# Expert leftovers in half tiles: two column groups on TensorE and a switch of seven arms

## The chip, the core and the metric

The kernel runs on one core of one Trainium2 chip. The metric is the device time of one execution in microseconds (us), lower being better; the profile adds one execution taken apart instruction by instruction. Engines are named as the profile names them: PE (TensorE, the matrix engine), PEld (its weight loads), DVE (VectorE), ACT (ScalarE), POOL (GpSimd) and SP (SyncE).

## The reference

The program is a strided sparse attention followed by a mixture of experts with one expert per token. Attention works on 8 batches, 8 heads, 576 positions and 64 channels a head; its output, reshaped to 8 x 576 rows of 512 floats, is the input of the expert layer:

```python
for b in range(B):
    prev_e = -1
    for s in range(S):
        fresh_e = int(np.argmax(logits[b, s]))
        if s == 0 or local_gate[b, s] < 0.5:
            e = fresh_e
        else:
            e = prev_e if prev_e >= 0 else fresh_e
        prev_e = e
        ls = logits[b, s] - logits[b, s].max()
        p = np.exp(ls)
        p /= p.sum() + 1e-09
        h = np.maximum(x[b, s] @ w1[e], 0.0)
        out[b, s] = p[e] * (h @ w2[e])
```

There are 8 experts; `w1[e]` is 512 x 1024 and `w2[e]` is 1024 x 512, all in float32. How many of the 4608 rows an expert gets depends on the data. Routing the given inputs by the reference gives 701, 469, 606, 495, 656, 452, 546 and 683 rows for experts 0 to 7.

## The kernel before, in words

Attention runs first, for about 190 us, and writes the rows to `xd` in DRAM. The router sorts rows by expert into tiles of 128 rows and keeps for each slot the row number and its gate. Then the expert stage runs; this is where the change lies.

**Units of work.** A *pair* is two tiles, 256 rows. `pair_hidden` and `pair_output` compute it with seven block products instead of eight, from sums of weights and of rows. In the hidden product (L807) the stationary operand is a 128 x 128 block of `w1` or of a weight sum, and the moving operand is 128 transposed rows. In the output product (L843) the hidden rows are stationary and 256 columns of `w2` move. A *single* (`single`) is one tile without the seven-product scheme: 32 matmuls of 128 columns for the hidden layer (L898) and 8 of 512 columns for the output (L909). A float32 matmul appears in the profile as two instructions, a transpose as one.

**Around a unit.** `gather` (L737) fetches its rows from `xd` by an indirect DMA that POOL issues, `scale` (L743) multiplies them by the gate on ACT, `turn` (L750, L751) transposes them on PE and copies them to `xt` on ACT, `row_sums` (L759) makes row sums for a pair on DVE, and `scatter` (L763) writes the result rows by an indirect DMA, again issued by POOL. `scale` and `turn` of the next unit are called inside the unit before it, so that the next rows are ready when it starts; a unit's transposes are therefore found among the matmuls of its predecessor.

**Four certain tiles, then a switch.** Every expert does its first two pairs (tiles 0 to 3). What lies past four tiles is known only at run time: `Router.arms` computes `pick`, the number of tiles past the fourth, held to 0 to 3. `choose` loads it into the registers of PE, ACT, DVE and POOL, and `rest` opens a switch in the middle of the second pair's output. The arms are written out in full: arm 0 nothing, arm 1 a single, arm 2 a pair, arm 3 a pair and a single. With the counts above, experts 0, 4 and 7 take arm 2, experts 2 and 6 take arm 1, and experts 1, 3 and 5 take arm 0. Expert 1 is finished before expert 0; the others follow in order.

**Order.** The order within each engine is that of the program text. Each unit calls `run(steps)` at set places; these steps are the DVE sums of the next expert's weights. The weights of the next expert are loaded by SP into one of two sets of buffers when the expert that used that set has finished with it. The rows of an expert's second pair and of its leftovers share one buffer; the first pair of the next expert has another.

Of the kernel before, what the change touches and what calls it, by code (L numbers as in the profile page):

```python
# [8 lines left out]
F32 = mybir.dt.float32  # L9
BF16 = mybir.dt.bfloat16  # L10
I32 = mybir.dt.int32
Act = mybir.ActivationFunctionType
Alu = mybir.AluOpType
# [5 lines left out]
P = 128  # L19
B, H, S, DH = 8, 8, 576, 64  # L20
D = H * DH
E, F = 8, 1024
DK, FK = D // P, F // P
N = B * S
# [16 lines left out]
HALF = P // 2  # L41


XT = 7
# [10 lines left out]

WARM = 14

ARMS = 4
SKIP = 8192
NEG = -8.0e9  # L60

# [21 lines left out]
class Unit:  # L83


    def __init__(self, b, pair, g):
        self.b, self.pair, self.g = b, pair, g
        self.local = pair < PAIRS // 2
        self.w, n = (LQ, LT) if self.local else (SQ, ST)
        self.kb = LK if self.local else SQ  # L90
        self.m = n // 2
# [356 lines left out]
class Router:  # L448
# [200 lines left out]
    def arms(self, bank):  # L649

        nc, pool, R, ident = self.nc, self.pool, self.R, self.ident
        f = lambda name, shape, t=F32: pool.tile(shape, t, name=name)
        ti, pk, ov, fine, bad = f("ti", [E, 1], I32), f("pk", [E, 1]), f("ov", [E, 2]), f("fine", [P, 2]), f("bad", [1, 1])

        nc.vector.tensor_scalar(ti, self.total[0:E], float(P), None, Alu.add)
        nc.vector.tensor_scalar(ti, ti, 7, None, Alu.arith_shift_right)
        nc.vector.tensor_copy(pk, ti)
        nc.vector.tensor_scalar(ov[:, 0:1], pk, -float(XT), 0.0, Alu.add, Alu.max)
        nc.vector.memset(ov[:, 1:2], 1.0)
        nc.vector.tensor_scalar(pk, pk, -4.0, 0.0, Alu.add, Alu.max)  # L660
        nc.vector.tensor_scalar(pk, pk, float(XT - 4), None, Alu.min)

        nc.vector.tensor_scalar(self.good, self.sums, 1.0 / TRUST, None, Alu.is_ge)
        nc.vector.scalar_tensor_tensor(self.good, self.sums, TRUST, self.good, Alu.is_le, Alu.mult)
        nc.vector.tensor_reduce(fine[:, 0:1], self.good.rearrange("p n h i -> p (n h i)"), axis=AX.X, op=Alu.min)
        nc.vector.memset(fine[:, 1:2], 1.0)
        yield
        ps = bank()
        nc.tensor.matmul(ps[0:1, 0:E], lhsT=pk, rhs=ident[0:E, 0:E], start=True, stop=True, skip_group_check=True)
        nc.tensor.matmul(ps[0:1, E:E + 1], lhsT=ov[:, 0:1], rhs=ov[:, 1:2], start=False, stop=True, skip_group_check=True)  # L670
        nc.vector.tensor_copy(self.pick, ps[0:1, 0:E])
        nc.tensor.matmul(ps[0:1, E + 1:E + 2], lhsT=fine[:, 0:1], rhs=fine[:, 1:2], start=False, stop=True,
                         skip_group_check=True)
        nc.vector.tensor_scalar(bad, ps[0:1, E + 1:E + 2], -1.0, float(P), Alu.mult, Alu.add)
        nc.vector.tensor_tensor(bad, ps[0:1, E:E + 1], bad, op=Alu.add)
        nc.vector.tensor_copy(self.flag, bad)
        yield
# [37 lines left out]
class Rows:  # L715


    def __init__(self, spot, tab, gi, cols, rows=N):
        self.x, self.xt, self.t = spot
        self.rows = rows  # L720
        self.n = len(cols)
        self.si = [tab[:, j, 0:1] for j in cols]
        self.gate = [tab.bitcast(F32)[:, j, 1:2] for j in cols]
        self.gi = [gi[:, j:j + 1] for j in cols]


class Experts:
# [6 lines left out]

    def gather(self, r):
        for i in range(r.n):
            self.nc.gpsimd.indirect_dma_start(out=r.x[:, i], out_offset=None, in_=self.xd[0:r.rows],  # L737
                                              in_offset=bass.IndirectOffsetOnAxis(ap=r.gi[i], axis=0))

    def scale(self, r):  # L740
        if r is not None:
            for i in range(r.n):
                self.nc.scalar.activation(r.x[:, i], r.x[:, i], Act.Copy, scale=r.gate[i])  # L743

    def turn(self, r, bank, only=None):
        if r is not None:
            for i in range(r.n) if only is None else [only]:
                ps = bank()[:, 0:DK * P].rearrange("p (k x) -> p k x", k=DK)
                for kk in range(DK):
                    self.nc.tensor.transpose(ps[:, kk], r.x[:, i, kk * P:(kk + 1) * P], self.ident)  # L750
                self.nc.scalar.copy(out=r.xt[:, i], in_=ps)  # L751

    def row_sums(self, r, which=range(4)):
        if r is not None and r.n == 2:
# [6 lines left out]
    def scatter(self, y, i, r):  # L761

        s = self.nc.gpsimd.indirect_dma_start(  # L763
            out=self.out, out_offset=bass.IndirectOffsetOnAxis(ap=r.si[i], axis=0),
            in_=y[:, i], in_offset=None, bounds_check=N - 1, oob_is_err=False)
        self.tc.declare_no_dep(s.ins, group="out", reason="scatters write different rows")
        self.tc.add_to_no_dep_group("out", s.ins)

    def run(self, ctx):
        nc, tc, w1, w2, router = self.nc, self.tc, self.w1, self.w2, self.router  # L770
        new = lambda name, bufs, **k: ctx.enter_context(tc.tile_pool(name=name, bufs=bufs, reuse_waits="tile", **k))
        wp, xp, up = new("wp", 1), new("xp", 1), new("up", 1)
        psx, psl, psm = new("psx", 2, space=PSUM), new("psl", 3, space=PSUM), new("psm", 1, space=PSUM)
# [3 lines left out]
        spots = [self.spot, (xp.tile([P, 2, D], F32, name="x1"), *self.spot[1:])]  # L777
        state = {"flip": 0}
# [4 lines left out]
        def run(steps):  # L783
            for do in steps.pop(0) if steps else []:
                do()
# [3 lines left out]
        def u(name, shape, pool=up):  # L789
            if name not in kept:  # L790
                kept[name] = pool.tile(shape, F32, name=name)
            return kept[name]

        relu = lambda o, i: nc.scalar.activation(o, i, Act.Relu)  # L794
        add = lambda o, i, p: nc.vector.tensor_tensor(o, p, i, op=Alu.add)  # L795
        hs, ys = [P, 4, P], [P, 256]
# [113 lines left out]
            nc.scalar.copy(out=y[:, 0], in_=ps)  # L910
            self.scatter(y, 0, r)

        def rows(spot, e, tiles):
            return Rows(spots[spot], router.tab, router.gi, [t * E + e for t in tiles])

        def load(e, w):
            w.load(nc, w1, w2, e)
            return w.sums(nc.vector)

        def slots(todo, counts):  # L920

            return [[todo.pop(0) for _ in range(min(n, len(todo)))] for n in counts]

        def output(r, w, h, nxt, steps):
            part1, part2 = pair_output(r, w, h)
            part1(steps)
            part2(nxt, steps)

        def choose(e):
            value = nc.values_load(router.pick[0:1, e:e + 1], engines=ENG, min_val=0, max_val=ARMS - 1,  # L930
                                   skip_runtime_bounds_check_because="held between 0 and 3")
            index = {n: value for n in ENG}
            tc.switch_hint(index, ARMS, label=f"expert{e}")
            return index

        def rest(e, w, spot, second, index, steps, nxt):

            if nxt is not None:
                self.gather(nxt)
            part1, part2 = pair_output(second, w, pair_hidden(second, w, steps))  # L940
            part1(steps)
            flip = state["flip"]

            for arm in tc.Switch(index, ARMS, hint=f"expert{e}"):
                state["flip"] = flip
                left = list(steps)
                more = []
                if arm > 1:
                    more.append(rows(spot, e, (4, 5)))
                if arm % 2:  # L950
                    more.append(rows(spot, e, (3 + arm,)))
                if more:
                    self.gather(more[0])
                part2(more[0] if more else nxt, left)
                for i, r in enumerate(more):
                    then = more[i + 1] if i + 1 < len(more) else nxt
                    if i + 1 < len(more):
                        self.gather(then)
                    if r.n == 1:
                        single(r, w, then, left)  # L960
                    else:
                        output(r, w, pair_hidden(r, w, left), then, left)
                while left:
                    run(left)
# [7 lines left out]
        more = router.scatters(1)  # L972
# [7 lines left out]
        arms = router.arms(bank)  # L980
        places[3].append(lambda: next(arms))
        places += [[lambda: next(arms), router.table, lambda: self.gather(second)]]
        h = pair_hidden(other, W[1], places)
        router.fetch()
        output(other, W[1], h, second, places)
        nxt = rows(1, 0, (2, 3))
# [4 lines left out]
        nxt = rows(0, 2, (0, 1))  # L991
        rest(0, W[0], 1, second, index, slots(sums, [0, 0, 1, 2, 1, 2, 2, 2, 2]) + [[f] for f in sums], nxt)
        for e in range(2, E):
            w, first, steps = W[(e + 1) % 2], nxt, []
            second = rows(1, e, (2, 3))
            self.gather(second)
            if e + 1 < E:
                steps = slots(load(e + 1, W[e % 2]), [0] * 5 + [1, 1, 1, 3] + [1] * 8 + [2])
                nxt = rows(0, e + 1, (0, 1))
            else:  # L1000
                nxt = None
            h = pair_hidden(first, w, steps)
# [466 lines left out]
```

## Time and profile before

| what | value |
|---|---|
| time, median of 9 runs | 744.96 us (741.96 to 752.91) |
| time of the profiled execution | 743.47 us |
| its span in the profile | 741.7 us |
| granted PE clock, mean | 0.961 |
| PE busy | 697.1 us, 94% of the span |
| PEld busy | 621.4 us, 84% |
| DVE busy | 380.9 us, 51% |
| ACT busy | 198.9 us, 27% |
| POOL busy | 134.1 us, 18% |
| DMA | 95.83 MB, mean 129 GB/s |

The profiled time is the span and 1.77 us around it. In the rows of the profile a group is the instructions of one source line, engine and shape: `L909 PE MATMUL mps<-w2t,h 128*128 128x512 f32 x32` is line 909, a matmul into the tile `mps`, with a 128 x 128 stationary block and 512 moving columns, executed 32 times. A matmul's own duration includes its latency; consecutive matmuls overlap, so what one costs in a stream is the distance between starts.

### The profile page before, as it was taken

The page shows a single profiled execution, that of the slowest core. Times are in us where ns is not written, and L with a number is a line of the kernel's source. Part 1 is how long each engine was busy: PE and PEld are TensorE (multiplying, and loading weights), DVE is VectorE, ACT ScalarE, POOL GpSimd, SP SyncE. Part 2 cuts the span into 40 slices and gives each one's busy share as a digit, 9 for nine tenths or more (in the row PEclk, how much of TensorE's full clock was granted, in tenths as well). Part 3 has the DMA queues.
Part 4 walks back from the last instruction along what each step waited for, and adds up shares of the span by engine and source line. Part 5 has one row for each costly group of instructions (what it writes and reads, how often), then busy time and mean ns, then how long its engine had stood idle before and what let it go on. Part 6 is the DMA issues. An engine that isn't in the chain of part 4 may idle for free.

```text
span 741.7 us, 15189 instructions
## 1 busy us (share of the span) xinstructions
PE 697.1 (94%) x6170; PEld 621.4 (84%) x6170; DVE 380.9 (51%) x896; ACT 198.9 (27%) x360; POOL 134.1 (18%) x150
## 2 busy tenths in 40 slices
PE   8999998697898999999999999999999999999993
PEld 5887886485697788999998999999999999889992
DVE  6667765372474523574563257366436646324341
ACT  3444452241320122221222222222222222212320
POOL 3000003204047221211121121131012112111001
PEclk9999999696998799999999999999999999999998
DMA  9798888722530024505222512520161442010000
GB/s 325 276 364 271 292 278 253 218 79 63 173 117 30 20 70 137 180 30 184 97 73 104 196 58 99 189 87 31 51 224 58 138 146 74 31 36 31 30 29 27
DMA packets 38057, 95.83 MB, mean 129 GB/s; under 512 B 5358, under 2 KB 14574, under 8 KB 37888
## 3 DMA queue, kind: packets, MB, share of 16 engines
q1 hardware_dynamic: 29616, 73.77, 29.0%
q0 software_dynamic: 7744, 20.08, 8.5%
q8 instruction: 64, 1.05, 0.6%
q14 instruction: 105, 0.86, 0.4%
q10 hardware_dynamic: 528, 0.07, 0.1%
HBM read 74.93 MB, written 20.02 MB: 128 GB/s over the span
## 4 chain that ended last, share of the span: by engine, by line
PE 90%; issue 3%; DVE 3%; DMA 1%; ACT 1%; POOL 1%; another core or an unknown queue 0%; POOLq 0%
PE lps L807 33%; PE mps L843 31%; PE sps L252 6%; PE vps L276 6%; PE tps L317 3%; PE xps L750 2%; PE lps L898 2%; PE mps L909 2%; PE sps L246 2%; PE vps L354 1%; PE tps L336 1%; DMA qk<-in_qks_dram 1%; DMA x<-xd,gi 1%; DVE xl L290 1%; DVE sums L289 0%
## 5 line engine op out<-in xcount | busy, mean ns | idle before, releaser
L807 PE MATMUL lps<-tt,ws 128*128 128x128 f32 x912 | 109.7, 275 | 3.8 <-issue 3.7
L807 PEld LDWEIGHTS lps<-tt,ws 128*128 128x128 f32 x912 | 105.6, 192 | 4.1 <-issue 3.9
L763 POOL DMA_INDIRECT out_dram<-y,tab x40 | 45.9, 1146 | 332.1 <-DVE y L795 273.4
L843 PE MATMUL mps<-wt,k 128*128 128x256 f32 x456 | 101.6, 379 | 0.0
L843 PEld LDWEIGHTS mps<-wt,k 128*128 128x128 f32 x456 | 86.6, 190 | 11.8
L795 DVE TENSOR_TENSOR h<-lps,u 128x512 f32<-128x512 f32 x57 | 39.4, 691 | 77.7 <-PE lps L807 69.9
L807 PE MATMUL lps<-xt,w1t 128*128 128x128 f32 x608 | 75.9, 279 | 0.0
L807 PEld LDWEIGHTS lps<-xt,w1t 128*128 128x128 f32 x608 | 74.1, 196 | 1.9 <-issue 1.0
L843 PE MATMUL mps<-w2t,h 128*128 128x256 f32 x304 | 72.5, 382 | 0.0
L577 POOL DMA_INDIRECT slots<-tok,idx x40 | 40.7, 1018 | 143.8 <-DVE tok L568 131.6
L843 PEld LDWEIGHTS mps<-w2t,h 128*128 128x128 f32 x304 | 56.9, 192 | 7.1
L252 PE MATMUL sps<-qk 64*128 64x96 f32 (+2 forms) x704 | 55.8, 286 | 5.8 <-issue 5.2
L737 POOL DMA_INDIRECT x<-xd,gi x40 | 39.6, 990 | 113.5 <-DVE tab L637 28.7
L252 PEld LDWEIGHTS sps<-qk 64*128 64x128 f32 (+2 forms) x704 | 45.4, 186 | 16.6 <-issue 14.4
L794 ACT ACTIVATE h<-h 128x512 f32<-128x512 f32 x57 | 35.9, 630 | 83.3 <-DVE h L795 81.3
L256 ACT ACTIVATE e<-sps 128x576 f32<-128x576 f32 (+1 forms) x64 | 41.4, 651 | 56.0 <-PE sps L252 34.3
L795 DVE TENSOR_TENSOR u<-lps,p 128x512 f32<-128x512 f32 x19 | 13.1, 692 | 58.3 <-PE lps L807 49.0
L807 PE MATMUL lps<-tt,w1t 128*128 128x128 f32 x304 | 40.8, 285 | 2.4 <-issue 2.4
L794 ACT ACTIVATE h<-lps 128x512 f32<-128x512 f32 x23 | 13.7, 597 | 104.8 <-PE lps L807 64.2
L807 PEld LDWEIGHTS lps<-tt,w1t 128*128 128x128 f32 x304 | 37.5, 198 | 4.4 <-issue 3.9
L807 PE MATMUL lps<-xt,ws 128*128 128x128 f32 x304 | 39.0, 284 | 0.0
L843 PE MATMUL mps<-w2t,k 128*128 128x256 f32 x152 | 37.6, 392 | 0.0
(214 smaller groups left out, 913.5 us busy)
## 6 DMA issues: line engine op xcount, KB each, us to landing
w1t<-in_w_dram SPq DMA_DIRECT2D x8, 2048.0 KB
w2t<-in_w_dram SPq DMA_DIRECT2D x8, 2048.0 KB
qk<-in_qkl_dram SPq DMA_DIRECT2D x16, 592.0 KB
qk<-in_qks_dram SPq DMA_DIRECT2D x16, 576.0 KB
vl<-in_vf_dram SPq DMA_DIRECT2D x8, 780.0 KB
vs<-in_vg_dram SPq DMA_DIRECT2D x8, 639.8 KB
xd<-xl SPq DMA_DIRECT2D x16, 288.0 KB
xd<-xs SPq DMA_DIRECT2D x64, 63.0 KB
```

Of the source, the lines that this page charges most:

```text
L246: nc.tensor.matmul(ps[0:GK, h, 0:n], lhsT=identb[0:GK, 0:GK], rhs=maskS[:, 0:n], start=True, stop=False, skip_group_check=True)
L252: nc.tensor.matmul(ps[0:m, h, c:c + w], lhsT=t[r, S + j * width:S + j * width + m], rhs=t[r, j * width:j * width + w], start=(u.local and ...
L256: nc.scalar.activation(e[0:kb, :, 0:n], ps[0:kb, :, 0:n], Act.Exp, bias=0.0, scale=1.0 / DH ** 0.5)
L276: nc.tensor.matmul(ps[a * HALF:(a + 1) * HALF, h, i], lhsT=u.e[0:m, h, q0:q0 + HALF], rhs=vt[0:m, j, 2 * i2 + h], start=(i == 0 and h == 0 ...
L317: nc.tensor.transpose(ps[:, t], src[:, t], ident)
L577: s = self.nc.gpsimd.indirect_dma_start(out=self.T, out_offset=bass.IndirectOffsetOnAxis(ap=self.idx[0:m, t, b:b + 1], axis=0), in_=self.t ...
L737: self.nc.gpsimd.indirect_dma_start(out=r.x[:, i], out_offset=None, in_=self.xd[0:r.rows], in_offset=bass.IndirectOffsetOnAxis(ap=r.gi[i], ...
L763: s = self.nc.gpsimd.indirect_dma_start(out=self.out, out_offset=bass.IndirectOffsetOnAxis(ap=r.si[i], axis=0), in_=y[:, i], in_offset=Non ...
L794: relu = lambda o, i: nc.scalar.activation(o, i, Act.Relu)
L795: add = lambda o, i, p: nc.vector.tensor_tensor(o, p, i, op=Alu.add)
L807: nc.tensor.matmul(ps[:, f], lhsT=m[:, kk, f * P:(f + 1) * P], rhs=v[:, kk], start=(start and f == 0 and kk == 0), stop=(kk == 1), skip_gr ...
L843: nc.tensor.matmul(ps[:, 0:256], lhsT=m[:, f], rhs=v[:, f], start=(start and f == 0), stop=(f == 3), skip_group_check=True)
```

## The change

`pick` now counts half tiles (64 rows) past the eighth, held to 0 to 6, and the switch has seven arms:

| arm | rows past 512 | work |
|---|---|---|
| 0 | none | nothing |
| 1 | up to 64 | a half |
| 2 | up to 128 | a single |
| 3 | up to 192 | a single and a half |
| 4 | up to 256 | a pair |
| 5 | up to 320 | a pair and a half |
| 6 | up to 384 | a pair and a single |

With the counts above, experts 0, 4 and 7 (189, 144 and 171 rows past 512) take arm 3, expert 2 (94 rows) takes arm 2, expert 6 (34 rows) takes arm 1, and experts 1, 3 and 5 take arm 0.

A *half* is a new unit of 64 rows. Its rows are the stationary operand in both products. Sixty-four stationary columns fill half of the array, so each product is split into two column groups: group 0 writes PSUM partitions 0 to 63 and group 1 partitions 64 to 127. In the hidden product group `g` has columns `512 g` to `512 g + 511` of `w1` as its moving operand; in the output product it has columns `256 g` to `256 g + 255` of `w2`. Between them the hidden rows are transposed on PE and copied back to SBUF by DVE. Gather, scale, transposes and scatter of a half work on 64 rows.

```diff
-ARMS = 4
+ARMS = 7
...
-        nc.vector.tensor_scalar(ti, self.total[0:E], float(P), None, Alu.add)
-        nc.vector.tensor_scalar(ti, ti, 7, None, Alu.arith_shift_right)
+        nc.vector.tensor_scalar(ti, self.total[0:E], float(HALF), None, Alu.add)
+        nc.vector.tensor_scalar(ti, ti, 6, None, Alu.arith_shift_right)
...
-        nc.vector.tensor_scalar(pk, pk, -4.0, 0.0, Alu.add, Alu.max)
-        nc.vector.tensor_scalar(pk, pk, float(XT - 4), None, Alu.min)
+        nc.vector.tensor_scalar(pk, pk, -8.0, 0.0, Alu.add, Alu.max)
+        nc.vector.tensor_scalar(pk, pk, float(ARMS - 1), None, Alu.min)
...
+        def half(r, w, nxt, steps):
+
+            self.scale(nxt)
+            a = psl.tile(hs, F32, name="lps").rearrange("p k x -> p (k x)")
+            for kk in range(DK):
+                for g in range(2):
+                    nc.tensor.matmul(a[g * HALF:(g + 1) * HALF], lhsT=r.xt[:, 0, kk, 0:HALF],
+                                     rhs=w.w1[:, kk, g * 512:(g + 1) * 512], start=(kk == 0), stop=(kk == DK - 1),
+                                     skip_group_check=True)
+            h, ht = u("h22", hs), u("h12", hs)
+            relu(h.rearrange("p k x -> p (k x)"), a)
+            self.turn(nxt, bank)
+            ps = psl.tile(hs, F32, name="lps")
+            for f in range(4):
+                nc.tensor.transpose(ps[:, f], h[:, f], self.ident)
+            nc.vector.tensor_copy(ht, ps)
+            self.row_sums(nxt)
+            flip = state["flip"] = 1 - state["flip"]
+            y = u(f"y{flip}", [P, 2, D])
+            b = u("mps0", [P, 512], psm)
+            for f in range(FK):
+                for g in range(2):
+                    nc.tensor.matmul(b[g * HALF:(g + 1) * HALF, 0:256], lhsT=ht[:, f % 4, f // 4 * HALF:(f // 4 + 1) * HALF],
+                                     rhs=w.w2[:, f, g * 256:(g + 1) * 256], start=(f == 0), stop=(f == FK - 1),
+                                     skip_group_check=True)
+            while steps:
+                run(steps)
+            for g in range(2):
+                nc.scalar.copy(out=y[0:HALF, 0, g * 256:(g + 1) * 256], in_=b[g * HALF:(g + 1) * HALF, 0:256])
+            self.scatter(y, 0, r)
...
-                if arm > 1:
+                if arm > 3:
                     more.append(rows(spot, e, (4, 5)))
+                if arm % 4 > 1:
+                    more.append(rows(spot, e, (4 + arm // 4 * 2,)))
                 if arm % 2:
-                    more.append(rows(spot, e, (3 + arm,)))
+                    more.append(rows(spot, e, (4 + arm // 2,), HALF))
...
-                    if r.n == 1:
+                    if r.m < P:
+                        half(r, w, then, left)
+                    elif r.n == 1:
                         single(r, w, then, left)
```

The rest of the diff passes the number of rows of a unit, 128 or 64, to `gather`, `scale`, `turn` and `scatter`.

## The prediction

> **What bounds the kernel now.** I read the page first: engine shares and the chain that ended last.
>
> ```profile
> span 741.7 us, 15189 instructions
> PE 697.1 (94%) x6170; PEld 621.4 (84%) x6170; DVE 380.9 (51%) x896; ACT 198.9 (27%) x360; POOL 134.1 (18%) x150
> PE 90%; issue 3%; DVE 3%; DMA 1%; ACT 1%; POOL 1%; another core or an unknown queue 0%; POOLq 0%
> ```
>
> PE carries 90% of the chain. A share is an average over stages, so next I read the chain in order of time where expert 2 ends. Columns are start, duration, what, number of instructions.
>
> ```profile
> 370.58 12.51 PE lps L807 x112
> 383.09 10.36 PE mps L843 x48
> 393.45 0.44 PE xps L750 x4
> 393.89 1.73 PE mps L843 x8
> 395.62 7.14 PE lps L898 x64
> 402.76 0.87 PE xps L750 x8
> 403.63 6.87 PE mps L909 x16
> ```
>
> Each piece starts where the last ended: from 297 us to the end of the last pair no other engine holds the chain. What counts here is the sum of PE's slots, so a unit's price is its slots plus any wait it brings. A pair costs 12.51 + 10.36 + 1.73 plus 0.87 for its own eight transposes, 25.47 us. The single costs 7.14 + 6.87 + 0.44 (four transposes, at 393.45), 14.45 us. The 0.87 at 402.76 belongs to the next pair and stays. Slots: 6.87 / 16 = 429 ns for 512 moving columns, 10.36 / 48 = 216 ns for 256, 7.14 / 64 = 112 ns for 128, 0.87 / 8 = 109 ns for a transpose.
>
> The half depends on two column groups running at once. Attention already does that twice, so I read PE's timeline there, and the row of line 336 (minimum, median and maximum ns, then its shapes).
>
> ```profile
> 65.31 0.77 PE L317 MATMUL tps<-ident,xs 128*128 128x128 f32 x5
> 66.00 1.62 PE L276 MATMUL vps<-vl,e 128*64 128x65 f32 x48
> 67.55 1.18 PE L336 MATMUL tps<-xT,wgs 128*32 128x504 f32 x16
> 68.66 0.43 PE L246 MATMUL sps<-maskS,identb 126*126 126x252 bf16 x2
> ```
>
> ```profile
> L336 PE MATMUL tps<-xT,wgs x128: 226/457/1049, 30.0 to 191.6; 128*32 128x504 f32 x64, 128*32 128x72 f32 x64
> ```
>
> L276 writes two groups of 64 columns. At about 60 ns a slot (112 ns less 63 columns at (216 - 112) / 128 ns) 48 of them would take 2.9 us one by one; the next line starts after 1.55. Its two groups share one moving block. L336 is nearer to the half: four groups of 32 columns, each with a different block of `xT` moving, half the instructions of 504 columns. One by one that is 8 x 423 + 8 x 65 ns = 3.9 us; the next line starts after 1.11. Four at a time it would be 0.98. So groups with different long moving operands do overlap fully.
>
> **The change, part by part.** *Streams of the half.* The hidden product is 8 matmuls, 16 instructions of 512 columns; two at a time, 8 x 429 ns = 3.44 us (6.87 one by one). The output product is 32 instructions of 256; two at a time, 16 x 216 = 3.45 us (6.91 one by one). I take the full overlap of L336. What neither row shows is a group that accumulates over its blocks; full-width streams (L898, L909) do so at an unbroken pace.
>
> The Trainium skill has a rule that speaks against this: "TensorE: Matmul & The Clock Gate", section "Measured speedup vs the span model", gives 2.38 times for three column groups of 32 with 512 columns, 0.79 of the ideal. At 0.79 of two the streams would take 8.7 us instead of 6.89, and the whole change would come to about -2.5 us. The row of L336, 3.9 / 1.11 = 3.5 times with four groups, is better than the rule, and I go by the row.
>
> *Changes between full width and groups.* Five transposes end their slots at 65.31 + 0.55 = 65.86 and L276 starts at 66.00; L276's 24 double slots end near 67.45 and L336 starts at 67.55; L336's 0.98 end at 68.53 and L246 starts at 68.66. That is 0.10 to 0.14 us each; I take 0.15, rounded up. A half has four (into and out of each product): 0.60 us.
>
> "TensorEngine Tiling (Array Packing)", section "Key Properties", says that a change of tiling mode drains TensorE. It gives no time; the rows show that such a drain is small, and with it at nothing the sum would gain 2.4 us.
>
> *Transposes.* Four for the hidden rows, 0.44 us. Its own four move 64 columns: between 0.24 (60 ns each) and 0.44 (their 128 stationary columns are those of the 109 ns row); I take 0.44.
>
> *The new wait.* The output product waits for DVE's copy of the transposed hidden rows (128x512), with only the output matmuls queued behind it on PE. Ends: 0.59 us (ACT's copy of that shape, L751) and 0.69 (DVE with 512 columns out of PSUM, L795); DVE's PSUM copies of 72 columns take 0.22 to 0.24, which agrees with the upper one. With 273 - 109 = 0.16 us until the last transpose is through and two handovers near 0.05, 0.95 us of idle PE. On DVE only the row sums of the next pair queue behind; they need 1.7 us and have 3.45.
>
> The first wait, for the relu, is 0.16 + 0.60 + 0.1 = 0.86 us and lies under the next pair's transposes (0.87 and a mode change). In expert 7 there is no next pair: uncovered it costs about 0.7.
>
> The half: 3.44 + 3.45 + 0.60 + 0.44 + 0.44 + 0.95 = 9.32 us.
>
> *The sum.* Experts 0 and 4: a pair becomes a single and a half, 14.45 + 9.32 - 25.47 = -1.70 each, -3.40. Expert 7: the same, +0.7 for the relu, and about -0.3 at the end, since its last scatter no longer queues behind another on POOL (0.92 us idle before it now) but waits for two ACT copies of 0.37: -1.30. Expert 6: 9.32 - 14.45 = -5.13. Expert 2 keeps its single, the rest their arm 0. Together -9.8 us.
>
> *Rows of the half after a single.* This gather is new in its place: POOL can issue it only after the second pair's last scatter, and ACT's `scale` for it stands ahead of the single's relus.
>
> ```profile
> 371.84 1.34 POOL L763 DMA_INDIRECT out_dram<-y,tab  x1 [1.58 <-issue]
> 373.49 0.99 POOL L737 DMA_INDIRECT x<-xd,gi  x1 [0.30 <-issue]
> 396.87 1.28 POOL L763 DMA_INDIRECT out_dram<-y,tab  x1 [1.14 <-issue]
> ```
>
> ```profile
> 257.70 4.19 DMA x<-xd,gi
> 295.57 1.79 issue
> ```
>
> Such a gather follows a scatter by 0.30 us, so at expert 2's times it would start at 398.45. The only wait for a gather that the chain shows lasted 4.19 us from its start: landed at 402.64, scaled by 403.4, with PE wanting it at 402.76. That instance followed another gather by 1.3 us, so this is the slow end: 0 to 0.65 us in experts 0, 4 and 7, at most 1.9. I take nothing, because no weight load runs then. A late `scale` holds the relus and the single's output too, but by no more than this.
>
> *Code.* Seven arms are more code. The one gap by instruction issue in this stage is the 1.79 us at 295.57, shortly after expert 1's arm. It may vanish or come once more: -1.8 to +1.8; I take none, since PE's branches end while matmuls are still queued.
>
> *Weights.* The next `w1` is released at the end of the half's hidden product, the next `w2` at its end, as in a single; their first uses come a pair later. The DVE steps left over in expert 0 (four, 2.7 us) move from the pair into the single, where DVE is otherwise idle. Both cost nothing; a DVE sum that waited for its weights would hold the copy of the half.
>
> **How it could go otherwise.** *The groups do not overlap.* Each half's streams then cost 13.78 instead of 6.89: 4 x 6.89 = 27.6 us dearer, +17.8 in all, 762.7 us. For it: the half's groups accumulate, which no grouped row does. Against it: L276 and L336. It decides from an overlap of 1.47 times: the gain is gone when each half is 9.8 / 4 = 2.46 us dearer, and 13.78 / (6.89 + 2.46) = 1.47. At about that overlap nothing changes, 745.
>
> *The rows come late.* The gather at its slow end in three experts, 1.9 us, and one more issue gap, 1.8: -6.1, 738.9 us. For it: ACT's order. Against: nothing else loads.
>
> *The arms are not the ones counted.* Expert 0 has 189 of the 192 rows that a single and a half hold. If rounding moved four rows, it would take the pair as before and lose 1.7 us of the gain: 736.8.
>
> **How the numbers follow.** The sum against the profiled execution is 743.47 - 9.8 = 733.7; that execution lies 1.5 below the median of the runs shown, so 744.96 - 9.8 = 735.1 us. Chances: forecast 0.83, late rows or another arm 0.09, partial overlap near break-even 0.03, no overlap 0.05. The fast end: own transposes 0.24 (-0.8), copy 0.59 (-0.4), mode changes at 0.11 (-0.6), the issue gap gone (-1.8): -13.4, 731.5. The slow end of the faster cases is 738.9; with a median that moves by about one microsecond the range is 731 to 740. What a measurement here can tell from no change is about 0.5%, 3.7 us: faster 0.92, same 0.03, slower 0.05.
>
> **What would show it.** Right: the half's hidden product as 16 instructions in about 3.4 to 3.7 us and its output as 32 in about the same; an idle PE of 0.9 to 1.0 us before the second; `L807 lps<-tt,ws` down from 912 to 768; experts 0 and 4 each 1.7 us shorter, expert 6 by 5.1. Wrong: starts of the two groups a full slot apart; PE waiting for the DMA or for ACT's `x` ahead of the half's transposes; issue gaps after the arms.

## The result and the profile after

| | kernel before | changed kernel |
|---|---|---|
| median | 745.94 us (739.74 to 752.91, 31 runs) | 736.52 us (732.84 to 741.64, 10 runs) |
| ratio of the two, 95% interval | | 0.9882 [0.9856, 0.9909] |
| profiled execution | 743.47 us, span 741.7 | 740.1 us, span 738.4 |
| expert stage, from expert 1's second pair to the end of the span | 475.23 us | 467.99 us |

The forecast was 735.1 us. The two profiled spans differ by only 3.3 us because the part ahead of the stage, in which the change alters only constants of the router, took 3.9 us longer in the profiled execution of the changed kernel: its stage begins at 270.39 us, that of the kernel before at 266.46. The stage is the part to compare, and there the difference is 7.24 us. The ratio stands for -8.8 us (-10.7 to -6.8), which holds both this and the predicted -9.8.

First the page of the changed kernel: span, engines, and shares of the chain that ended last.

```profile
span 738.4 us, 14832 instructions
PE 684.6 (93%) x6034; PEld 587.0 (79%) x6034; DVE 353.2 (48%) x843; ACT 195.2 (26%) x357; POOL 135.2 (18%) x150
PE 83%; issue 7%; DVE 5%; another core or an unknown queue 2%; ACT 1%; POOL 1%; DMA 1%; DVEq 0%; POOLq 0%
```

PE has 136 instructions and 12.5 us of busy time less. ("Issue" is time in which an engine waited for nothing that the profile shows.) That PE's share of the chain falls from 90% to 83% does not mean that PE lost its place: at the very end the chain now runs through POOL's scatters and its pauses between them (11.80 and 8.35 us of "issue" in the last 32 us), under which PE computes the last single and the last half. In POOL's own timeline these two pauses end when ACT has copied the result of the single and of the half. In section 5 the sum-weight matmuls of the pairs went from 912 to 768, as foreseen: three pairs are gone.

```profile
L807 PE MATMUL lps<-tt,ws 128*128 128x128 f32 x768 | 91.7, 275 | 1.3 <-issue 0.7
```

Next the chain in order of time where expert 0's leftovers run (start, duration, what, number of instructions). This is the first half on the chip.

```profile
322.04 7.14 PE lps L898 x64
329.19 0.39 PE xps L750 x4
329.58 7.06 PE mps L909 x16
336.64 3.58 PE lps L919 x16
340.22 1.03 PE xps L750 x8
341.25 0.45 PE lps L927 x4
341.70 0.02 issue
341.73 0.70 DVE h L928
342.43 0.04 issue
342.47 3.70 PE mps L935 x32
346.17 0.02 issue
346.19 0.38 ACT y L941
346.57 0.04 issue
346.61 12.77 PE lps L807 x112
```

Read it piece by piece. The hidden product (L919) has 16 instructions in 3.58 us and the output product (L935) 32 in 3.70: two column groups at a time, and the streams accumulate. The relu's wait is not in the chain, since the next pair's transposes (1.03 us) cover it. DVE's copy (L928) holds PE for 0.77 us. And there is a piece that the prediction does not have: between L935 and the next pair's first L807 PE waits for ACT's copy of the half's own result (L941), though that pair does not use it; and L807 then takes 12.77 us instead of 12.51.

A second new wait stands where an expert ends with arm 0:

```profile
461.48 1.73 PE mps L843 x8
463.21 0.56 issue
463.77 4.14 PE lps L807 x35
```

In the kernel before, L807 follows L843 there at once:

```profile
459.71 1.73 PE mps L843 x8
461.44 12.50 PE lps L807 x112
```

The view of PE's waits (engine, line, what it waited for; us in total, times, longest) from 290 us on sums the new ones; the kernel before has only 1.8 us of issue in this view.

```profile
PE mps L935 <- DVE h L928: 3.1, 4, 0.8
PE lps L807 <- issue: 1.4, 3, 0.6
PE lps L807 <- ACT y L941: 1.4, 3, 0.5
PE lps L927 <- ACT h L794: 0.7, 1, 0.7
PE lps L807 <- DVE u L795: 0.6, 1, 0.6
```

The first row and the fourth are the prediction's waits for the copy and for expert 7's uncovered relu. The other three are not in it. The last row stands behind expert 1's arm: DVE has 5.06 us of issue there, and PE waits for its sum `u`, where the kernel before had PE's own pause of 1.79 us.

### The profile page after: what moved, and what is told of

Same layout as the page of the kernel before. It is cut to its first block, busy times and chain, and to the rows that moved or that the text cites. A ratio compares the mean times of both kernels' runs of the same rounds, so it can differ in the third digit from the quotient of the medians.

```text
span 738.4 us, 14832 instructions
## 1 busy us (share of the span) xinstructions
PE 684.6 (93%) x6034; PEld 587.0 (79%) x6034; DVE 353.2 (48%) x843; ACT 195.2 (26%) x357; POOL 135.2 (18%) x150
## 3 DMA queue, kind: packets, MB, share of 16 engines
q8 instruction: 66, 1.08, 0.6%
## 4 chain that ended last, share of the span: by engine, by line
PE 83%; issue 7%; DVE 5%; another core or an unknown queue 2%; ACT 1%; POOL 1%; DMA 1%; DVEq 0%; POOLq 0%
PE lps L807 26%; PE mps L843 26%; PE vps L276 6%; PE sps L252 6%; PE tps L317 3%; PE lps L898 3%; PE mps L909 3%; PE xps L750 2%; PE sps L246 2%; PE mps L935 2%; PE lps L919 1%; PE vps L354 1%; PE tps L336 1%; DVE xl L290 1%
## 5 line engine op out<-in xcount | busy, mean ns | idle before, releaser
L807 PE MATMUL lps<-tt,ws 128*128 128x128 f32 x768 | 91.7, 275 | 1.3 <-issue 0.7
L807 PEld LDWEIGHTS lps<-tt,ws 128*128 128x128 f32 x768 | 88.6, 192 | 1.7 <-issue 0.8
L843 PE MATMUL mps<-wt,k 128*128 128x256 f32 x384 | 85.6, 379 | 0.0
L843 PEld LDWEIGHTS mps<-wt,k 128*128 128x128 f32 x384 | 72.9, 190 | 9.9
L807 PE MATMUL lps<-xt,w1t 128*128 128x128 f32 x512 | 64.5, 280 | 2.5 <-ACT y L941 1.4
L807 PEld LDWEIGHTS lps<-xt,w1t 128*128 128x128 f32 x512 | 62.0, 196 | 5.9 <-ACT y L941 2.8
L795 DVE TENSOR_TENSOR h<-lps,u 128x512 f32<-128x512 f32 x48 | 33.2, 691 | 67.8 <-PE lps L807 58.5
L843 PE MATMUL mps<-w2t,h 128*128 128x256 f32 x256 | 61.0, 382 | 0.0
L843 PEld LDWEIGHTS mps<-w2t,h 128*128 128x128 f32 x256 | 47.9, 192 | 5.9
L795 DVE TENSOR_TENSOR u<-lps,p 128x512 f32<-128x512 f32 x16 | 11.1, 692 | 57.9 <-PE lps L807 29.2
L743 ACT ACTIVATE x<-x,tab 128x512 f32<-128x512 f32 (+1 forms) x40 | 27.2, 718 | 41.2 <-DMA x<-xd,gi 27.4
L807 PE MATMUL lps<-xt,ws 128*128 128x128 f32 x256 | 33.1, 285 | 4.7 <-DVE h L795 4.7
L807 PEld LDWEIGHTS lps<-xt,ws 128*128 128x128 f32 x256 | 31.5, 201 | 5.7 <-DVE h L795 5.6
L289 DVE RECIPROCAL sums<-vps 128x6 f32<-128x6 f32 (+1 forms) x64 | 12.1, 189 | 48.9 <-PE vps L276 26.7
```

The source lines that it names most:

```text
L743: self.nc.scalar.activation(r.x[0:r.m, i], r.x[0:r.m, i], Act.Copy, scale=r.gate[i][0:r.m])
L807: nc.tensor.matmul(ps[:, f], lhsT=m[:, kk, f * P:(f + 1) * P], rhs=v[:, kk], start=(start and f == 0 and kk == 0), stop=(kk == 1), skip_gr ...
L843: nc.tensor.matmul(ps[:, 0:256], lhsT=m[:, f], rhs=v[:, f], start=(start and f == 0), stop=(f == 3), skip_group_check=True)
```

## The experiments

They ran on two chips on which the kernel before takes 710 to 711 us, so each is told as a ratio to that kernel on the same chip, and the changed kernel was run again on one of the two. The last column is the stage as defined above, in the one profiled execution of each. The changed kernel's own two profiles agree there to 0.44 us (467.99 and 467.55, on different chips), while the ratios are known to 0.3 or 0.4%, 2 to 3 us. So small differences are read from the units in the profile; they hold for the execution that was profiled.

| run | ratio, 95% interval | stage, us |
|---|---|---|
| changed kernel again | 0.9896 [0.9865, 0.9927] | 467.55 |
| groups one after the other | 1.0150 [1.0116, 1.0184] | 485.70 |
| second result copy on DVE | 0.9888 [0.9850, 0.9926] | 471.13 |
| seven arms, work of before | 1.0070 [1.0039, 1.0102] | 481.12 |
| half in expert 6 alone | 0.9984 [0.9958, 1.0011] | 475.89 |
| order that covers waits | 0.9861 [0.9817, 0.9905] | 464.42 |
| kernel before with three dead arms | 0.9975 [0.9951, 1.0000] | 473.94 |
| four arms with the half | 0.9913 [0.9883, 0.9943] | 469.29 |
| transposes into another tile | 0.9881 [0.9845, 0.9917] | 466.88 |
| one result copy | 0.9897 [0.9861, 0.9933] | 466.33 |
| all waits out | 0.9896 [0.9855, 0.9936] | 465.58 |
| half in expert 6 alone, no weight loads | 0.9939 [0.9909, 0.9968] | 471.20 |

**Do the groups carry the gain?** Theory: the half pays because its two groups run side by side. The edit gives each group its whole product before the other's:

```diff
-            for kk in range(DK):
-                for g in range(2):
+            for g in range(2):
+                for kk in range(DK):
```

and the same in the output product.

> All matmuls of the half's column group 0 stand before all of group 1, so that no two neighbours can run side by side; nothing else changes. Theory (the half is cheap because its two groups overlap): the hidden product goes from 3.6 us to 6.6 to 6.9 and the output product from 3.7 to 6.7 to 6.9 in each of four halves, 24 to 27.6 us in all, 760 to 764 us, slower than the kernel before. Rival (the gain is from fewer rows and fewer pair products, whatever the groups do): less than 5 us dearer than the changed kernel, still below 742.

The changed kernel's gain turns into a loss of 1.5%. In the chain of this run the two products of a half are:

```profile
300.18 5.35 PE lps L919 x16
307.77 6.33 PE mps L935 x32
```

They take 4.40 us more than in the changed kernel; four halves make 17.6, and the stage is 18.15 longer. So without the overlap there is no gain. The loss is smaller than expected (1.0150 of 746 us is 757, not 760 to 764), since the overlap did not vanish entirely: both products stay below the 6.9 us of a full sequence, because PE began group 1 while group 0 was still running (the last section).

**The wait for ACT's copy.** Theory: PE waits for a count of ACT's instructions which, behind the switch, is the same for all arms. A single has one ACT instruction behind the copies of the next rows, a half has two. The edit moves the second of them to DVE:

```diff
-            for g in range(2):
-                nc.scalar.copy(out=y[0:HALF, 0, g * 256:(g + 1) * 256], in_=b[g * HALF:(g + 1) * HALF, 0:256])
+            nc.scalar.copy(out=y[0:HALF, 0, 0:256], in_=b[0:HALF, 0:256])
+            nc.vector.tensor_copy(y[0:HALF, 0, 256:], b[HALF:, 0:256])
```

> The second of the half's two output copies moves from ACT to DVE, so that only one ACT instruction follows the copy of the next pair's rows. Theory (the next pair's first matmul waits for an ACT count that stands one instruction before the end of the arm, and the half has two instructions there): the 0.44 us between the half's last matmul and the next L807 goes away in experts 0, 4 and 6, 1.2 to 2.1 us less with what follows, about 735 us. Rival (the pause is PE's change from two groups back to full width): the pause stays, 736.5 us.

The wait went, as the theory says: from start to start a half fell from 10.04 to 9.50 us in all three places. But the ratio did not move beyond its interval, and in the profiled execution, the slowest of its six, the stage became 3.6 us longer. DVE now ends the arm, and its next instruction behind the arm came late:

```profile
504.09 0.07 DVE y L941
504.16 8.25 issue
512.41 0.02 DVEq L795
512.43 0.04 issue
512.47 0.70 DVE u L795
513.17 0.04 issue
513.22 7.25 PE lps L807 x48
```

From DVE's branch to its next instruction 8.31 us passed here, 5.83 and 3.35 at the other two exits; PE had to wait for the sum `u`, and this pair took 29.70 us instead of 25.57. Of these 4.1 us 1.6 came after the wait: the granted clock was 0.50 from 513.43 us for 3.4 us, and the 48 matmuls behind `u` took 7.25 us where the changed kernel's took 5.62. A wait was traded for a late start.

**Is it the switch itself?** Four runs ask whether seven arms cost something by their mere size. The first takes the changed kernel's switch but rounds odd counts of halves up to the old work:

```diff
-                if arm > 3:
+                tiles = (arm + 1) // 2
+                if tiles > 1:
                     more.append(rows(spot, e, (4, 5)))
-                if arm % 4 > 1:
-                    more.append(rows(spot, e, (4 + arm // 4 * 2,)))
-                if arm % 2:
-                    more.append(rows(spot, e, (4 + arm // 2,), HALF))
+                if tiles % 2:
+                    more.append(rows(spot, e, (3 + tiles,)))
```

> Seven arms chosen by half tiles, but an odd number of half tiles is rounded up to whole tiles: the work of every expert is that of the kernel before. Theory (more code costs nothing by itself): 745 to 747 us, same as the kernel before. Rival (each arm of the longer switch is fetched later): one more issue gap of about 1.8 us in several experts, 749 us or more.

It came out slower by 0.7%, as the rival had it. Its chain has three pauses of PE's issue, 2.55 us at 260.36, 1.12 at 357.12 and 1.43 at 561.56. The pairs in which they stand are 7.5 us above the usual; the kernel before has one such pair, 1.95 us above. The difference, 5.6 us, is 0.8% of 710 and accounts for the loss; whether the longer switch causes the pauses is what the next runs ask. The second run kept the half only for expert 6 and gave experts 0, 4 and 7 their pair back (`arm > 2` for the pair, `arm in (2, 6)` for the single, `arm in (1, 5)` for the half).

> Three half tiles are done as a pair again, so that only expert 6 takes a half. Theory (by the unit times of the profile after): expert 6 alone gives 4.5 us, 741.4 us; the three experts with a single and a half give the rest, about 1.1 to 1.7 us each. Rival (the single and half gains nothing, since the gather or the mode changes take it back): as fast as the changed kernel, 736.5.

Here too less was measured than expected, -1.1 us. In the profile expert 6 does gain its 4.5 us (60.88 us for its second pair, the half and the next pair, where the kernel before takes 65.39 with a single), but one pause takes it back. It stands 12 matmuls behind expert 3's exit, just after SP had issued the loads of the next weights (`w1` at 421.4, `w2` at 425.7 us):

```profile
425.71 1.34 PE lps L807 x12
427.05 3.78 issue
430.83 13.87 PE lps L807 x100
```

The pause costs more than its own length: this pair took 31.95 us instead of 25.47, 6.5 us more. A hundred of these matmuls usually take 11.2 us. Here the granted clock was 0.50 from 429.4 to 436.2 us, and until 436 the matmuls started 213 ns apart instead of 112. Of the pauses of PE's issue named here, the three above 2.3 us each bring 3.4 to 6.8 us at half clock, and none of those up to 1.79 us does.

The third is the kernel before with `ARMS = 7` and three arms that are never taken:

> The kernel before with three more arms (pair, pair and single twice) that are never taken: the count of tiles and the arms 0 to 3 are as before. Theory (a longer switch costs by its length alone, as the 0.7% of the seven arms with the old work says): 0.4 to 0.7% slower than the kernel before. Rival (that 0.7% came from where the chosen arms lie, or from the way the arms are numbered): within 0.2% of the kernel before.

Arms that are never taken cost nothing: 0.9975, if anything below 1, so the theory of that run failed. The fourth is the changed kernel with only the four arms that this input needs (larger experts go to the general path):

> The changed kernel with its first four arms only (nothing, half, single, single and half); an expert with more than 704 rows would raise the flag that repeats everything on the general path, and none has. Theory (the length of the switch costs about 5 us): 4 to 5 us less than the changed kernel, ratio about 0.982. Rival (length costs nothing): the ratio of the changed kernel, 0.988.

No gain from the shorter switch as a whole either. This profile, too, has pauses of issue on PE (2.38 us at 260.42, 0.95 at 421.11); the two pairs are 4.5 us longer by them than in the changed kernel. Against that its end is shorter: from the end of PE's last matmul to the end of the span 8.5 us pass instead of 11.5. Arm 3, which experts 0, 4 and 7 take, is the last arm here, with no other arm behind it. After its exits POOL went on within 0.5 us, where it needs 6.0, 5.8 and 2.5 us in the changed kernel. As to the pauses, they belong to no number of arms; they fall differently in every program, the kernel before included (1.79 us).

**Where do the pauses come from?** The last run of this question takes the kernel with the 3.78 us pause and leaves out the weight loads of experts 3 to 7:

```diff
-                steps = slots(load(e + 1, W[e % 2]), [0] * 5 + [1, 1, 1, 3] + [1] * 8 + [2])
+                steps = slots(W[e % 2].sums(nc.vector), [0] * 5 + [1, 1, 1, 3] + [1] * 8 + [2])
```

> The kernel with a half in arm 6's place only (arm 3 as a pair) without the weight loads of experts 3 to 7: they compute with the weights of experts 0 and 2, so the output is not the reference's; every other instruction stays. The load of expert 2's weights stays in too, as a control. With loads this kernel came out at 0.9984 of the kernel before and its profile had an issue gap of 3.78 us on PE at 427 us, 12 matmuls behind an arm's exit and just after a weight load was issued. Theory (the gaps are instruction fetches that queue behind weight loads): without loads the gaps of over 0.5 us behind experts 2 to 6 vanish, ACT's and DVE's first instructions after a branch come within about 2 us instead of 2.4 to 8.3, and the time falls by 4 to 5 us, ratio about 0.992 to 0.993. Rival (fetching after a far branch is that slow by itself, wherever the code lies): the gaps stay, ratio 0.998. Waits for weights cannot explain a difference, since the chain shows none.

The chain at the same place, behind expert 3's exit:

```profile
426.12 1.56 PE lps L807 x14
427.68 0.01 issue
427.69 11.21 PE lps L807 x98
```

The long pause is gone, the stage is 4.7 us shorter, and the rival's 0.998 lies outside the interval. The pause is one event, and the intervals of the two runs (0.9958 to 1.0011 with loads, 0.9909 to 0.9968 without) still touch. POOL shows the link more often. With the loads, 5.5 to 6.4 us passed between its branch at an arm's exit and its next instruction at the six exits near which weights load, and 3.06 at expert 6's, where nothing is loaded. Without them it was 5.90 at the exit beside the one load that stayed in, and 2.6 to 2.8 at the other six. Two points of the theory missed. One pause of 1.09 us remained (at 545.95), without any load. And where ACT was late behind a branch, its first instruction came after 2.15 to 2.75 us where 2 was expected; with the loads the same branches show 2.16 to 2.78, so they made 0.2 us of difference there at most. So weight loads lengthen POOL's way out of an arm by about 3 us, and the longest pause of PE went with them. That it is the fetching of instructions that waits behind the loads fits this, but is argued; what decides which exit is hit stays open.

**An order that covers the waits.** The relu is shared by ACT and DVE, the next rows' second tile is transposed behind the hidden rows instead of ahead of them, the copy is in two pieces, and the output blocks go in the order in which the pieces arrive:

```diff
-            relu(h.rearrange("p k x -> p (k x)"), a)
-            self.turn(nxt, bank)
+            relu(hf[:, 0:256], a[:, 0:256])
+            nc.vector.tensor_scalar(hf[:, 256:], a[:, 256:], 0.0, None, Alu.max)
+            self.turn(nxt, bank, 0)
...
+            nc.vector.tensor_copy(ht[:, 0:2], parts[0][:, 0:2])
+            self.turn(nxt, bank, 1)
+            nc.vector.tensor_copy(ht[:, 2:4], parts[1][:, 0:2])
-            for f in range(FK):
+            for f in (0, 4, 1, 5, 2, 6, 3, 7):
```

On the same chip the changed kernel was run again, unchanged:

> The half's two waits are covered: relu is split between ACT and DVE by columns, the next pair's first four transposes stand before those of the hidden rows and its last four after them, the copy of the transposed hidden rows goes in two pieces of 256 columns, and the output product takes the blocks in the order of the pieces. Theory (PE's 0.77 us before the output product, and in expert 7 also 0.7 us before the transposes, are idle time of the path): 0.6 us less in experts 0, 4 and 6 and 0.7 to 1.2 in expert 7, 2.5 to 3 us in all, 0.35 to 0.4% below the changed kernel. Rival (ACT and DVE reach the next pair later and it waits there instead): no gain.

> The changed kernel itself, next to the kernel before on the same chip and beside the three below. Theory: a ratio of 0.988 as in the result, whatever the chip. Rival (the gain of the result was partly the luck of issue gaps): between 0.99 and 1.0.

The changed kernel's 0.9896 [0.9865, 0.9927] holds the 0.988 of its theory and reaches into the rival's range, so it does not decide between them; the profile has to. In the run with the new order PE's wait for the copy vanished. A half takes 9.54 us (9.60 in expert 6) instead of 10.04 and the last one, from its first matmul's start to its last's, 8.39 instead of 9.09, and the stage is 3.1 us shorter than that of the changed kernel, the shortest of all runs. By the ratios, 0.9861 beside 0.9896, the two intervals overlap, so this is the best kernel found and likely a little better, not more.

**The two waits at the join, one by one.** The join is the place behind the switch where the arms meet again. First, the half's hidden rows are transposed into a tile of the output product instead of a buffer of `lps`:

```diff
-            ps = psl.tile(hs, F32, name="lps")
+            ps = u("mps1", [P, 512], psm).rearrange("p (k x) -> p k x", k=4)
```

> The half's hidden rows are transposed into the PSUM tile mps1 instead of a buffer of lps. Theory (the wait at the switch's join): in the changed kernel DVE's copy of the transposed rows is the last reader of a buffer of lps, so the first L807 after every switch waits for DVE as well, whatever arm ran; after arm 0 that makes PE wait for DVE's last sum of the pair, 0.72 us at the ends of experts 3 and 5. With the copy reading mps1 that wait is gone: these two pairs go back from about 26.2 to about 25.5 us, the 0.56 us of issue and the idle ahead of it vanish from the chain, and the time falls by about 1.5 us, ratio to the kernel before about 0.987 to 0.988 beside the 0.9896 of the changed kernel on this chip; within the scatter of one comparison, so the units of the profile decide. Rival (PE arrives late after arm 0 because its own instructions come late): the units stay at 26.2, ratio 0.9896.

The waits at arm 0 are gone. The chain at expert 3's exit:

```profile
426.50 1.73 PE mps L843 x8
428.23 3.35 PE lps L807 x30
```

The pairs ahead of the exits of experts 3 and 5 are at 25.47 us from start to start (26.20 and 26.19 when the changed kernel was run again, on the other chip), and expert 0's second pair is 0.48 shorter. That is 1.9 us; about 0.8 of it came back in the next pair, with a pause of issue of 0.64 at 431.58. Next, in all halves but the last, one ACT copy of 128 partitions for both groups and two scatters into halves of rows:

```diff
-            for g in range(2):
-                nc.scalar.copy(out=y[0:HALF, 0, g * 256:(g + 1) * 256], in_=b[g * HALF:(g + 1) * HALF, 0:256])
-            self.scatter(y, 0, r)
+            nc.scalar.copy(out=y[:, 0, 0:256], in_=b[:, 0:256])
+            for g in range(2):
+                self.scatter_part(y, g, r)
```

> Except in the last unit, one ACT copy takes both column groups of a half's output out of PSUM (128 partitions, 256 columns) and two scatters write the two halves of the rows, with row numbers 2 n and 2 n + 1 in a view of 256 columns. Theory (the join of ACT's counts): a half has two ACT instructions behind the copies of the next rows where a single has one, and the next pair's first L807 waits for the first of them; with one copy it does not wait. The 0.44 us between the half's last matmul and that L807 goes, and ACT's copy p1 is no longer late by 0.10: three halves at 9.6 instead of 10.04 us and the pairs behind them at 25.47 instead of 25.57, together -1.6 us, ratio about 0.987. The second scatter costs POOL about 1 us per half, off the path. Rival (the wait is for the end of the arm's ACT work in any case, or PE needs that time to get its instructions): the half stays at about 10.0, as an issue gap or a wait for the one copy, and the ratio at 0.990.

Three halves at 9.50 us: the wait is for the count of ACT's instructions, as the theory says, and it is worth 0.54 a half. The pairs behind them stayed at 25.57, against the expectation. Why they take 0.10 more than other pairs stays open. The time as a whole did not show the gain, 0.9897. This run also names the wait at arm 0, which the changed kernel's chain calls "issue": it is DVE's last sum of the pair. (The edit moves the lines: L807 is here the line of DVE's sums, L795 in the changed kernel.)

```profile
423.79 0.44 DVE y L807
424.23 0.24 issue
```

At last everything together, with the relu on ACT alone:

> All at once: transposes of the hidden rows into mps1 and mps2 in two pieces, each copied by DVE when it is there, relu in two pieces on ACT, the next rows' second tile transposed behind the hidden rows as cover for the copy, output blocks in the order 0 4 1 5 2 6 3 7, one ACT copy and two scatters as in the run beside it. By theory the terms add: about 0.5 us less per half for the covered copy (three halves) and 0.7 in the last one, as measured before for that order, 0.54 per half for the join with ACT, 1.5 for the join with DVE: -5.3 us against the changed kernel, ratio about 0.982. The half should measure about 9.1 us. Rival (each wait that goes uncovers the next one: PE's issue or ACT's late p1): less than half of it, ratio 0.986 to 0.988, with issue gaps or waits of the same length in the same places.

A half now takes 8.82 us (expert 6: 8.87), less than expected, and the last one 8.39. The stage is 2.0 us shorter than the changed kernel's, not 5.3, and the ratio is the same, 0.9896, where the theory had 0.982 and the rival 0.986 to 0.988. Less than half came, as the rival said. The chain shows where it went. In this kernel L954 is the half's output product, L819 the pair's hidden product and L826 ACT's copy of its first part.

```profile
302.59 3.63 PE mps L954 x32
306.21 0.02 issue
306.24 0.04 ACT y L964
306.28 4.90 issue
311.18 0.04 ACTq L826
311.22 0.04 issue
311.26 0.59 ACT p L826
311.86 0.04 issue
311.90 7.41 PE lps L819 x64
```

PE goes from L954 to the next pair without a wait, but ACT needs 4.90 us from its exit to its next instruction, and PE waits for that copy `p` 5 us into the pair: 0.42 us here, 0.83 at expert 4's half, and 1.45 and 0.60 us of issue elsewhere. Each wait that is taken out of the half brings the late start behind the switch to the front.

## Why the prediction was right

The mechanism and the sign were right, the time came out 1.4 us above the forecast and inside the range. One microsecond of the 1.4 is the kernel before, whose median is 745.94 over 31 runs where the forecast started from 744.96. The terms, against the stage of the profile shown above:

| step | predicted, us | measured, us |
|---|---|---|
| experts 0 and 4, each | -1.70 | -1.08 |
| expert 6 | -5.13 | -4.51 |
| expert 7 | -1.30 | -1.51 |
| exits by arm 0 of experts 3 and 5 | 0 | +2.03 |
| pause behind expert 1's arm, with 0.08 of the pair ahead | 0 (-1.8 to +1.8) | -1.09 |
| sum | -9.83 | -7.24 |

**The streams** were the deciding step, and it held. The two products take 3.58 + 3.70 us, the change of mode adds 0.19 to the single's output ahead of them (7.06 against 6.87) and 0.16 to the transposes between them (1.03 against 0.87): 7.63 us where the sum had 6.89 + 0.60 = 7.49. In the trace the starts of the two groups lie 5 to 7 ns apart and the next two follow after 429 ns, or 216 in the output. Accumulation does not disturb the overlap. The serial run shows that the first rival, had its condition held, would have ended slower, as it said.

The figure of the Trainium skill against which the row of L336 was weighed ("TensorE: Matmul & The Clock Gate", "Measured speedup vs the span model", 2.38 times for three groups) does not carry over to these products: the estimate from it, at 0.79 of the ideal, was 8.7 us for the streams. They took 7.28, where their slots one by one would be 13.78: 1.89 times, 0.95 of the ideal.

**The small terms** were close. The wait for the copy: 0.77 us for 0.95. Four transposes of hidden rows 0.45 for 0.44, of own rows 0.39 for 0.44. Expert 7's uncovered relu 0.7 for 0.7. Without the wait for ACT the half is 7.63 + 0.45 + 0.39 + 0.77 = 9.24 us, beside the 9.32 of the sum.

**What was missed.** Each half ahead of another expert is 0.62 us dearer than predicted. 0.54 of that is the join with ACT: the single-copy run takes exactly this much away. The prediction named the scatter's wait for two ACT copies, but did not ask which later instruction on PE waits for ACT's count behind the switch. The second is the join with DVE. Because the copy of the hidden rows is the last reader of a buffer of `lps`, the next pair's first L807 waits for DVE in every arm, and after arm 0 it waits for DVE's last sum: the exits of experts 3 and 5 took 2.03 us more in this profile (1.6 when the kernel was run again). The run with the transposes in `mps1` shows the cause for 1.45 us of this, in the two pairs ahead of the exits; the rest lies in the pairs behind them and stays open. The step of the prediction that failed is "Expert 2 keeps its single, the rest their arm 0": the work of arm 0 was kept, its waits were not.

**What came out as foreseen for its reason.** The rows of the half after a single were on time: from the gather's issue to `scale` 3.07 us passed in expert 7, and at 336.64 and 529.54 L919 follows L909 without a wait. Weights held nothing up. **Code** was entered at nothing with a range: arms that are never taken are indeed free (one run), but the range for the pauses, 1.8 us, was too narrow for programs of this kind, as 3.78 in one and 5.1 in three pauses of another showed. It also left out the half clock that follows a long one. In the changed kernel itself the loss behind expert 1's arm fell from 1.95 to 0.94 us above the usual pair, a wait for DVE in place of PE's pause; that was luck and not part of the reasoning. So the small miss in the time hides two errors that partly cancel: joins of about +3.7 us left out, and 1.3 us gained elsewhere.

## What to carry to other kernels

A remainder that needs only half of the stationary columns can run as two column groups with different moving operands at nearly half the time, also with accumulation; order the instructions so that the groups alternate. When a unit is added to one arm of a switch, look at the waits of the first instructions behind the switch: counts there must hold for every arm, so an extra last instruction, or a buffer whose last reader is now another engine, is paid for by arms that did not change. And when an engine's last work moves to the end of an arm, its next instruction may come late, here by 2.4 to 8.3 us, so work that others wait for is better not put last there.

## What the hardware showed that was not expected

PE starts matmuls of another column group ahead of its program order. In the serial run group 1's first matmul instruction started 1.775 us after group 0's first, 6 ns behind group 0's fifth of eight; three pairs of starts followed, and the last four of group 1 ran alone. In the output product, 16 instructions a group, it started beside group 0's thirteenth. Both times four instructions were left, so the look-ahead is four instructions there. The section "What overlaps and what doesn't" of the Trainium skill's "TensorE: Matmul & The Clock Gate" has matmuls strictly in program order; for these two groups the starts in the trace say otherwise.

Starting again behind an arm that has other arms behind it in the program is slow, and slower while weights load. POOL needed 2.6 to 2.8 us at such exits without loads and 5.5 to 6.4 with them, but 0.5 us where the arm was the last of the switch. ACT needed 2.15 to 2.75 us in the run without loads; behind a half with one result copy, whose exit comes some 3.6 us after a 2 MB load of `w1` was issued, 4.94 and 5.35. DVE needed 8.31 and 5.83 us at two such exits and 3.35 at the one without loads. The run without loads shows the link for POOL and for the longest pause of PE; for ACT and DVE it is argued from these exits.

A long pause of PE is paid for twice. At pauses of 2.38, 2.55 and 3.78 us of issue the granted clock went to 0.50 for 3.4, 3.4 and 6.8 us, and in the longest case this cost 2.7 us on top of the 3.78.
